# Moving work across the two ends of the attention stage in a fused attention, MLP and expert kernel

## The chip, the core and the metric

The kernel runs on one core of one Trainium2 chip. The metric is the device time of one execution in microseconds (us). Before the change the median of 3 runs is 1051.84 us (1050.31 to 1052.88). One further execution was taken with the hardware profiler: its own time is 1050.91 us, and the span that the trace covers is 1049.2 us.

## What is computed

Three layers run one after the other on 4 x 576 = 2304 tokens of width 512.

1. Attention with 8 heads of width 64 for each of 4 batches, causal, with a memory branch beside it:

```python
a = softmax(causal(q @ k.T / 8));  local = a @ v
q_p = phi(q)                       # phi(x) = max(x, 0) + exp(min(x, 0))
mem = (q_p @ M_prev) / (q_p @ z_prev + 1e-6)
g = sigmoid(beta)                  # one gate for each head
x = g * mem + (1 - g) * local
```

2. A gated MLP: `xn = x / sqrt(mean(x*x) + 1e-6) * rms_g`, then `(silu(xn @ w_gate) * (xn @ w_val)) @ w_out`, with an inner width of 1536. The three weight matrices arrive as 64-bit floats.

3. A mixture of 8 experts, each token going to its best one (512 to 1024 to 512), scaled by the router's probability and an output gate.

## The kernel before, in words

**Stages.** `attention` (L222) runs first. The MLP runs in `moe` (L923) over 5 blocks of 512 tokens (the last has 256), each in 12 steps f = 0..11 over 128 of the 1536 inner columns. The experts follow. Every large fp32 product is made of three fp32r products (high times high, high times low, low times high), so each weight tile is split into a rounded half and a rest: a copy and a subtraction.

**Attention.** Heads are taken two batches at a time (bp 0 and 1), so there are 16 heads n = 0..15, each in five units: four `Pair`s of 64-row blocks and one `Last`. The loop over units (L477 to L508) writes the order of the work by hand: at unit u it scores unit u on TensorE (PE) and takes the negative row maximum on VectorE (DVE), turns the weights of unit u-2 (PE transposes, ScalarE (ACT) copies), makes the exponentials of unit u (`soft`, ACT), and multiplies unit u-3 by v (`value`). After a head's last `value`, `add` scales the result (DVE, tile tm) and adds it to x on GpSimd (POOL). `recall` adds the memory branch at units 3 to 5 and at three units of every ten. `core.chain(True)` (L1152) holds this order on PE, DVE, ACT and POOL: an instruction there starts only after the one written before it on the same engine. The queue that issues DMAs (SP) is not held so; its order, and all orders after attention, are set by a scheduler at build time.

**Generators.** Side work is written as Python generators in a list `work`; at the end of each unit every generator is advanced by one `yield`. `load(n)` (L239) fetches q and k of head n and scales q by 0.125 on ACT, `phi(n)` (L248) fetches q again and makes phi(q) (DVE, ACT, DVE) for two heads, `piece` (L153) decodes one of 21 tiles of 64-bit weights to fp32 and stores it to DRAM (wgvd, woutd), `dense.weights` (L545) fetches the gate and value weights of one MLP step from wgvd and splits them, `rms` (L446) makes the mean squares of finished x rows (ACT, one row tile of 128 tokens at a time), the inverse root (POOL) and the scaled rows (DVE), and stores them to xd in DRAM. Before the change `rms` runs inside attention only for row tiles 0, 1, 2, 3 and 8 of bp 0 (`EARLY`); the other 4 row tiles of bp 0 and all 9 of bp 1 come in `late` (L513), which `moe` advances.

**The beginning.** Before unit 0 the DMAs of head 0, phi 0, the first v, beta and head 1 are issued (L278 to L285). Head 1's scaling on ACT (L246) and the gates `ig` = 1 + exp(-beta) and `io` = 1 + exp(beta) (L287 to L290) stand ahead of unit 0 on ACT and DVE. `ig` is first read by `recall` at unit 3, `io` by `add` after unit 4. phi's input tile q has one buffer.

**The end.** At the last unit of head 15, `route_constants` (L114) builds index constants on POOL and DVE: masks, ramps, and `ids`, 36 iotas of one column each. The weights of MLP step 0 are split during heads 12 and 13. After attention its SBUF pools are given back, and the pools of `moe` take the same memory. There `prepare(k)` (L949) fetches what step k needs: the weights (from step 1 on; from step 7 on `Late` decodes them in place) through tiles of tag `wo`, which has two buffers, and the output weights (`outw`, L937) through the same two buffers. `late` is advanced ten times before step 0 (L968), and four times in each step of block 0.

Of the kernel before, what the change touches and what calls it, by code (L numbers as in the profile page):

```python
# [17 lines left out]
P = 128  # L18
S = 576
# [17 lines left out]
EARLY = (0, 1, 2, 3, 8)  # L37
# [76 lines left out]
def route_constants(nc, cp, c):  # L114
# [28 lines left out]
    for bp in range(2):  # L143
        for t in range(9):
            for u in range(2):
                k = 8 * bp + t if t < 8 else 16 + bp
                nc.gpsimd.iota(ids[64 * u:64 * u + 64, k:k + 1], pattern=[[0, 1]], base=(2 * bp + (u ^ (t & 1))) * S + 64 * t, channel_multiplier=1)
# [74 lines left out]
def attention(ctx, nc, tc, ins, c, g8, rp, ps, xd, side):  # L222
# [16 lines left out]
    def load(n):  # L239

        qt = pl.tile([P, 2, S], F32, tag='qk', bufs=4, name='qt')
        heads.append(qt)
        nc.sync.dma_start(qt, qk[n // 8, n % 8].rearrange('b d (a s) -> (b d) a s', a=2))
        for _ in range(3 if n > 1 else 0):
            yield
        nc.scalar.mul(qt[:, 0], qt[:, 0], 0.125)  # L246

    def phi(n):  # L248

        q = pl.tile([P, 2, S], F32, tag='qs', bufs=1, name='q')  # L250
        nc.sync.dma_start(q, qs[n // 4, n % 4].rearrange('b p s -> p b s'))
        ph = pl.tile([P, 2, S], F32, tag='ph', name='ph')
        phis.append(ph)
        yield
        if n:
            yield
        nc.vector.tensor_scalar(ph, q, 0.0, None, op0=ALU.min)
        yield
        nc.scalar.activation(ph, ph, AF.Exp)
        yield  # L260
        nc.vector.scalar_tensor_tensor(ph, q, 0.0, ph, op0=ALU.max, op1=ALU.add)
# [18 lines left out]
    work = [phi(0)]  # L280
    next(work[0])
    values(0)
    nc.sync.dma_start(bt, ins['beta'].partition_broadcast(P))
    for _ in load(1):
        pass  # L285

    nc.vector.tensor_scalar(bt, bt, 80.0, -80.0, op0=ALU.min, op1=ALU.max)  # L287
    for t, sign in ((ig, -1.0), (io, 1.0)):
        nc.scalar.activation(t, bt, AF.Exp, scale=sign)
        nc.vector.tensor_scalar(t, t, 1.0, None, op0=ALU.add)  # L290
# [12 lines left out]
    def start(n):  # L303
# [7 lines left out]
        H.av = ps.tile([P, 8, 64], F32, tag='av', name='av')  # L311
        return H

    class Pair:
# [35 lines left out]
        def value(self):  # L350
            H, i = self.H, self.i
            for j in range(2):
# [5 lines left out]
    class Last:  # L358
# [35 lines left out]
        def value(self):  # L394
# [7 lines left out]
            if H.hh == 7 and H.bp == 0:  # L402
                work.append(rms(0, EARLY))

# [41 lines left out]
    def rms(bp, ts, ps=None):  # L446

        n = len(ts)
        x = [xs[bp][t // 4][:, t % 4] for t in ts]
        early = bp == 0 and ts[0] == 0  # L450
        pool = cp if early else rp
        ss, y, z = (pool.tile([P, 9], F32, tag=n + 'e' * early, name=n)[:, :len(ts)] for n in ('ss', 'y', 'z'))
# [3 lines left out]
        for t in range(n):  # L456
            sq = cp.tile([P, 512], F32, tag='sq', name='sq') if early else ps.tile([P, 512], F32, tag='m', name='sq')
            nc.scalar.activation(sq, x[t], AF.Square, accum_out=ss[:, t:t + 1])
            yield
        nc.vector.tensor_scalar(ss, ss, 1.0 / 512, 1e-6, op0=ALU.mult, op1=ALU.add)  # L460
        nc.gpsimd.tensor_tensor(y, ss, state['mhalf'][:, :n], op=ALU.pow)
# [51 lines left out]
    def late(ps):  # L513
        yield from rms(0, [t for t in range(9) if t not in EARLY], ps)
        yield from rms(1, range(9), ps)
# [407 lines left out]
def moe(ctx, tc, c, dense, X, late, g8, ps, ins, woutd, wr, rowd, wf, out):  # L923
# [25 lines left out]
    def prepare(k):  # L949
        if k < len(steps):  # L950
            bi, f = steps[k]
            if W[f] is None:
                for _ in dense.weights(f, g8 if f == 1 else w8, 'g8' if f == 1 else 'w8', pw, 'wo'):
                    pass
# [9 lines left out]
    ex = Experts(nc, c, wf, rowd, out, g8, w8, pw, pe, ps, cp)  # L964
    prepare(0)
    for p in range(2):
        decode.load(p)
    for _ in range(10):  # L968
        next(late)
# [10 lines left out]
    for k, (bi, f) in enumerate(steps):  # L980
# [7 lines left out]
        g = [ps.tile([P, 512], F32, tag='gv', bufs=3, name='gv')[:, :w] for _ in range(2)]  # L988
# [117 lines left out]
def body(tc, ins, out):  # L1106
# [4 lines left out]
    with ExitStack() as ctx:  # L1111
# [13 lines left out]
        with ExitStack() as c1:  # L1125
# [4 lines left out]
            def side(n, j):  # L1130
# [15 lines left out]
                if n == 12:  # L1146
                    w.append(dense.weights(0, g8, 'g8', pd, 'dw'))
                if n == 15:
# [53 lines left out]
```

## Time and profile before

| what | value |
|---|---|
| median of 3 runs | 1051.84 us |
| the profiled execution | 1050.91 us |
| its span | 1049.2 us |
| PE, DVE, ACT, POOL busy, share of the span | 93%, 66%, 54%, 24% |
| chain that ended last, PE's share | 62% |

Times within the trace are microseconds from the start of its span. In a timeline row the columns are start, duration, engine, source line, operation, what is written <- what is read, shape and count; brackets give the idle time of that engine just before, and what ended it. SPq is the queue that issues DMAs. PEld is the weight load that goes with a matmul. Most instructions carry line L57, since a helper there records them, so a row is found by its tile names: m are row maxima, mx those of a `Last`, a the attention weights, bt beta, qt the q and k of a head, ph phi(q), tm and x the attention output, Wf the split MLP weights, gv the first MLP product, dw and wo the tiles that weights are fetched to. A busy PE is not a PE at its peak, since matmuls overlap.

### The profile page before, as it was taken

What the parts mean: (1) busy time and instruction counts of PE and PEld (TensorE: products, weight loads), DVE (VectorE), ACT (ScalarE), POOL (GpSimd) and SP (SyncE); (2) the same over time, 40 slices, a digit from 0 to 9 for tenths busy, and PEclk for the clock granted to TensorE, in tenths of its full rate; (3) what the DMA queues carried; (4) which work ended last, traced back from release to release, by engine and by line L of the source; (5) the groups of instructions that cost most, each with busy time, mean ns of one, the idle gap of its engine ahead of it and who ended that gap; (6) DMA issues with size and microseconds to landing.
All of it is one profiled execution on the core that took longest, in us unless ns stands there. A gap on an engine that the chain in (4) does not pass through costs nothing.

```text
span 1049.2 us, 18572 instructions
## 1 busy us (share of the span) xinstructions
PE 974.8 (93%) x6727; PEld 751.7 (72%) x6727; DVE 693.7 (66%) x1261; ACT 571.3 (54%) x1113; POOL 251.1 (24%) x266
## 2 busy tenths in 40 slices
PE   5999998886989999999999999999879999999996
PEld 3666665554667777887788778888757888777785
DVE  3788888875987644234523354247687988888885
ACT  4788887766343332222222222235447888888885
POOL 1222222325555311110111112114003222222101
PEclk9999999998999999999999999999999999999999
DMA  8366556304754411021211112134134453387323
GB/s 275 100 203 193 180 180 223 101 25 161 261 170 123 135 44 61 31 71 32 69 31 51 31 61 67 35 96 147 60 101 154 128 195 125 101 297 272 101 101 98
DMA packets 51279, 128.21 MB, mean 122 GB/s; under 512 B 9965, under 2 KB 10477, under 8 KB 50672
## 3 DMA queue, kind: packets, MB, share of 16 engines
q1 hardware_dynamic: 47664, 116.48, 34.0%
q0 software_dynamic: 3520, 10.51, 3.1%
q8 instruction: 54, 0.88, 0.3%
q14 instruction: 41, 0.34, 0.1%
HBM read 160.50 MB, written 22.04 MB: 174 GB/s over the span
## 4 chain that ended last, share of the span: by engine, by line
PE 62%; DVE 12%; issue 8%; DMA 8%; ACT 6%; POOL 3%; SPq 0%; POOLq 0%; ACTq 0%; DVEq 0%
PE gv L57 22%; PE acc L57 11%; PE y L57 8%; PE h L57 7%; PE sc L57 3%; PE av L57 2%; PE tr L57 2%; DMA dw<-wgvd 2%; DMA out_dram<-ys,to 2%; DVE m L57 1%; PE tp L57 1%; ACT whl L850 1%; PE htp L57 1%; PE mp L57 1%; DVE whl L851 1%
## 5 line engine op out<-in xcount | busy, mean ns | idle before, releaser
L57 PE MATMUL gv<-xh,Wf 128*128 128x512 f32 (+1 forms) x960 | 290.1, 375 | 16.3 <-ACT Wf L57 7.8
L851 DVE TENSOR_TENSOR whl<-raw,whl 128x1024 fp32r<-128x1024 f32 x173 | 204.2, 1219 | 29.6 <-ACT whl L850 29.0
L57 PEld LDWEIGHTS gv<-xh,Wf 128*128 128x128 f32 x960 | 174.7, 189 | 51.9 <-ACT Wf L57 8.2
L850 ACT CAST whl<-raw 128x1024 fp32r<-128x1024 f32 x176 | 177.0, 1059 | 15.0 <-PE h L57 5.0
L57 PE MATMUL gv<-xl,Wf 128*128 128x512 f32 (+1 forms) x480 | 177.4, 370 | 0.0
L1007 POOL TENSOR_TENSOR sl<-th,sh 128x512 fp32r<-128x512 f32 (+1 forms) x58 | 72.3, 1246 | 313.0 <-ACT sh L1006 308.4
L57 PE MATMUL y<-whl,hh 128*128 128x512 f32 x528 | 137.7, 401 | 0.6 <-DVE whl L851 0.6
L57 PE MATMUL h<-whl,xgh 128*128 128x512 f32 x352 | 117.3, 401 | 2.7 <-DVE whl L851 2.0
L57 PEld LDWEIGHTS y<-whl,hh 128*128 128x128 f32 x528 | 97.4, 190 | 21.3 <-DVE whl L851 1.6
L57 PEld LDWEIGHTS gv<-xl,Wf 128*128 128x128 f32 x480 | 90.8, 189 | 14.2
L1006 ACT CAST sh<-th 128x512 fp32r<-128x512 f32 (+1 forms) x60 | 34.6, 576 | 121.2 <-DVE th L1003 121.2
L943 DVE TENSOR_TENSOR wol<-wo,woh 128x512 fp32r<-128x512 f32 x60 | 47.4, 789 | 67.6 <-ACT woh L942 67.5
L57 PE MATMUL acc<-woh,sh 128*128 128x512 f32 x216 | 87.1, 403 | 0.2
L57 PE MATMUL acc<-wol,sh 128*128 128x512 f32 x216 | 85.6, 396 | 0.0
L57 ACT ACTIVATE a<-sc,m 128x128 f32<-128x128 f32 (+3 forms) x128 | 66.9, 532 | 30.0 <-DVE m L57 18.6
L57 PE MATMUL acc<-woh,sl 128*128 128x512 f32 x216 | 78.8, 398 | 3.8 <-POOL sl L1007 3.8
L1002 DVE SCALAR_TENSOR_TENSOR th<-th,gv 128x512 f32<-128x512 f32 (+1 forms) x60 | 37.9, 632 | 63.4 <-ACT th L1001 63.3
L57 PEld LDWEIGHTS h<-whl,xgh 128*128 128x128 f32 x352 | 64.6, 188 | 21.1 <-DVE whl L851 7.4
L1001 ACT ACTIVATE th<-gv 128x512 f32<-128x512 f32 (+1 forms) x60 | 33.2, 554 | 83.0 <-PE gv L57 79.1
L942 ACT CAST woh<-wo 128x512 fp32r<-128x512 f32 x60 | 37.2, 620 | 64.8 <-PE acc L57 43.3
L1003 DVE TENSOR_TENSOR th<-th,gv 128x512 f32<-128x512 f32 (+1 forms) x60 | 37.9, 632 | 49.6 <-PE gv L57 49.0
L57 PE MATMUL h<-whl,xgl 128*128 128x512 f32 x176 | 68.7, 392 | 0.0
(252 smaller groups left out, 1571.3 us busy)
## 6 DMA issues: line engine op xcount, KB each, us to landing
raw<-in_wf_dram SPq DMA_DIRECT2D x168, 512.0 KB
wo<-woutd SPq DMA_DIRECT2D x60, 256.0 KB
raw<-in_wgv_dram SPq DMA_DIRECT2D x24, 512.0 KB
qt<-in_qk_dram SPq DMA_DIRECT2D x16, 576.0 KB
raw<-in_wout_dram SPq DMA_DIRECT2D x12, 512.0 KB
q<-in_qs_dram SPq DMA_DIRECT2D x8, 576.0 KB
xd<-x SPq DMA_DIRECT2D x18, 256.0 KB
rowd<-xr SPq DMA_DIRECT2D x4, 1028.0 KB
```

The lines of the kernel that those rows point to most:

```text
L57: i = call(*args, **kw).ins
L850: nc.scalar.copy(w[:, 0], src)
L851: (nc.gpsimd if k in pool_k else nc.vector).tensor_tensor(w[:, 1], src, w[:, 0].bitcast(F32), op=ALU.subtract)
L942: nc.scalar.copy(woh, wo)
L943: nc.vector.tensor_tensor(wol, wo, woh.bitcast(F32), op=ALU.subtract)
L1001: nc.scalar.activation(th, g[0], AF.Tanh, scale=0.5)
L1002: nc.vector.scalar_tensor_tensor(th, th, 1.0, g[0], op0=ALU.add, op1=ALU.mult)
L1003: nc.vector.tensor_tensor(th, th, g[1], op=ALU.mult)
L1006: nc.scalar.copy(sh, th)
L1007: (nc.vector if f >= 10 and bi == last else nc.gpsimd).tensor_tensor(sl, th, sh.bitcast(F32), op=ALU.subtract)
```

## The change

- The first scaling of head 1 waits three units, as for the later heads, so it stands behind unit 2's start; its DMA is issued before those of v and beta. phi's input tile q gets the pool's two buffers instead of one.
- The gates become a generator: the clamp and the two exponentials at unit 1, the two additions at unit 2.
- A head's PSUM tile av is created at its first `value` instead of at its start, which puts it behind the score tiles in PSUM; `moe` creates its first two gv tiles ahead of everything else.
- `rms(0)` takes all 9 row tiles of bp 0 inside attention; `late` is left with bp 1, and the ten advances ahead of step 0 are gone.
- The weights of MLP step 1 are fetched and split inside attention, one head after those of step 0.
- `route_constants` moves from head 15 to head 9, and `ids` is made by 12 iotas instead of 36.

```diff
     ids = t('ids', [NT], I32)
     for bp in range(2):
-        for t in range(9):
-            for u in range(2):
-                k = 8 * bp + t if t < 8 else 16 + bp
-                nc.gpsimd.iota(ids[64 * u:64 * u + 64, k:k + 1], pattern=[[0, 1]], base=(2 * bp + (u ^ (t & 1))) * S + 64 * t, channel_multiplier=1)
+        for u in range(2):
+            o, r = (2 * bp + u) * S, ids[64 * u:64 * u + 64]
+            nc.gpsimd.iota(r[:, 8 * bp:8 * bp + 8:2], pattern=[[P, 4]], base=o, channel_multiplier=1)
+            nc.gpsimd.iota(ids[64 * (1 - u):128 - 64 * u, 8 * bp + 1:8 * bp + 8:2], pattern=[[P, 4]], base=o + 64, channel_multiplier=1)
+            nc.gpsimd.iota(r[:, 16 + bp:17 + bp], pattern=[[0, 1]], base=o + 512, channel_multiplier=1)
...
-        for _ in range(3 if n > 1 else 0):
+        for _ in range(3 if n else 0):
             yield
         nc.scalar.mul(qt[:, 0], qt[:, 0], 0.125)
...
-        q = pl.tile([P, 2, S], F32, tag='qs', bufs=1, name='q')
+        q = pl.tile([P, 2, S], F32, tag='qs', name='q')
...
-    work = [phi(0)]
-    next(work[0])
+    work = [phi(0), load(1)]
+    for w in work:
+        next(w)
     values(0)
     nc.sync.dma_start(bt, ins['beta'].partition_broadcast(P))
-    for _ in load(1):
-        pass
-
-    nc.vector.tensor_scalar(bt, bt, 80.0, -80.0, op0=ALU.min, op1=ALU.max)
-    for t, sign in ((ig, -1.0), (io, 1.0)):
-        nc.scalar.activation(t, bt, AF.Exp, scale=sign)
-        nc.vector.tensor_scalar(t, t, 1.0, None, op0=ALU.add)
+
+    def gates():
+
+        yield
+        yield
+        nc.vector.tensor_scalar(bt, bt, 80.0, -80.0, op0=ALU.min, op1=ALU.max)
+        for t, sign in ((ig, -1.0), (io, 1.0)):
+            nc.scalar.activation(t, bt, AF.Exp, scale=sign)
+        yield
+        for t in (ig, io):
+            nc.vector.tensor_scalar(t, t, 1.0, None, op0=ALU.add)
+
+    work.append(gates())
+    next(work[-1])
...
-        H.av = ps.tile([P, 8, 64], F32, tag='av', name='av')
+        H.av = None
...
             H, i = self.H, self.i
+            if H.av is None:
+                H.av = ps.tile([P, 8, 64], F32, tag='av', name='av')
...
             if H.hh == 7 and H.bp == 0:
-                work.append(rms(0, EARLY))
+                work.append(rms(0))
...
-    def rms(bp, ts, ps=None):
-
-        n = len(ts)
+    def rms(bp, ps=None):
+
+        ts, n = (0, 1, 2, 3, 8, 4, 5, 6, 7), 9
...
-        yield from rms(0, [t for t in range(9) if t not in EARLY], ps)
-        yield from rms(1, range(9), ps)
+        yield from rms(1, ps)
...
-                for _ in dense.weights(f, g8 if f == 1 else w8, 'g8' if f == 1 else 'w8', pw, 'wo'):
+                for _ in dense.weights(f, w8, 'w8', pw, 'wo'):
...
     ex = Experts(nc, c, wf, rowd, out, g8, w8, pw, pe, ps, cp)
+    first = [ps.tile([P, 512], F32, tag='gv', bufs=3, name='gv') for _ in range(2)]
     prepare(0)
     for p in range(2):
         decode.load(p)
-    for _ in range(10):
-        next(late)
     prepare(1)
...
-        g = [ps.tile([P, 512], F32, tag='gv', bufs=3, name='gv')[:, :w] for _ in range(2)]
+        g = first if k == 0 else [ps.tile([P, 512], F32, tag='gv', bufs=3, name='gv')[:, :w] for _ in range(2)]
...
-                if n == 12:
-                    w.append(dense.weights(0, g8, 'g8', pd, 'dw'))
-                if n == 15:
+                if n in (12, 13):
+                    w.append(dense.weights(n - 12, g8, 'g8', pd, 'dw'))
+                if n == 9:
                     route_constants(core, cp, c)
```

## Rows read from the trace of the kernel before

**Rows 1.** The profile page, busy time of each engine over the span.

```profile
PE 974.8 (93%) x6727; PEld 751.7 (72%) x6727; DVE 693.7 (66%) x1261; ACT 571.3 (54%) x1113; POOL 251.1 (24%) x266
```

**Rows 2.** Busy time by stretch: attention, block 0, and 10 us of it.

```profile
core 0: us, PE busy (x) PEld busy (x) DVE busy (x) ACT busy (x) POOL busy (x), PEclk, DMA share, GB/s
13.00:241.20 228.20, 208.09 (x3068) 138.23 (x3068) 182.29 (x389) 172.75 (x507) 64.27 (x102) 0.99 0.49 159
246.60:363.80 117.20, 99.54 (x417) 75.94 (x416) 92.92 (x142) 47.97 (x89) 54.29 (x39) 0.97 0.54 177
250.00:260.00 10.00, 4.46 (x11) 3.13 (x12) 8.13 (x15) 8.24 (x21) 3.29 (x3) 0.66 0.67 248
```

**Rows 3.** Timeline of all engines, the first 30 us.

```profile
6.44 0.39 PE L57 MATMUL sc<-maskb,identb 128*128 128x128 bf16 x2
...
9.41 0.17 DVE L57 TENSOR_SCALAR bt<-bt 128x8 f32<-128x8 f32 x1 [5.00 <-DMA bt<-in_beta_dram]
...
12.00 0.68 ACT L57 ACTIVATE qt<-qt 128x576 f32<-128x576 f32 x1 [6.24 <-DMA qt<-in_qk_dram]
...
12.99 0.42 DVE L57 TENSOR_REDUCE m<-sc 128x2 f32<-128x256 f32 x1
...
15.80 0.69 DVE L57 TENSOR_REDUCE m<-sc 128x2 f32<-128x512 f32 x1 [0.86 <-PE sc L57]
...
18.68 0.38 SPq L251 DMA_DIRECT2D q<-in_qs_dram  x1
...
24.15 0.76 DVE L57 TENSOR_SCALAR ph<-q 128x1152 f32<-128x1152 f32 x1 [1.95 <-DMA q<-in_qs_dram]
...
24.83 0.75 DVE L57 TENSOR_REDUCE mx<-scl 128x2 f32<-128x576 f32 x1
```

**Rows 4.** Timeline of POOL, heads 5, 7, 9 and 11 added to x, and attention's end.

```profile
101.49 1.88 POOL L57 TENSOR_TENSOR x<-x,tm 128x256 f32<-128x256 f32 x3 [1.55 <-DVE tm L57]
...
128.04 1.87 POOL L57 TENSOR_TENSOR x<-x,tm 128x256 f32<-128x256 f32 x3 [1.59 <-DVE tm L57]
...
156.07 2.32 POOL L57 TENSOR_TENSOR x<-x,tm 128x256 f32<-128x256 f32 x3 [4.47 <-DVE tm L57]
...
184.01 1.89 POOL L57 TENSOR_TENSOR x<-x,tm 128x256 f32<-128x256 f32 x3 [4.58 <-DVE tm L57]
...
236.91 6.62 POOL L57 IOTA ids<- 64x1 int32 x36
...
244.85 1.71 POOL L57 TENSOR_TENSOR x<-x,tm 128x256 f32<-128x256 f32 x3
```

**Rows 5.** Groups by line and form, DVE and ACT, 100 to 246 us; last numbers: busy, mean ns.

```profile
L57 DVE TENSOR_SCALAR x<-x,y 128x512 f32<-128x512 f32 x5 | 3.6, 715 | 0.0
...
L57 DVE TENSOR_TENSOR Wf<-dw,Wf 128x512 fp32r<-128x512 f32 x1 | 0.7, 693 | 0.0
L57 DVE CAST Wf<-dw 128x512 fp32r<-128x512 f32 x1 | 0.4, 417 | 0.0
L57 DVE CAST lane<-lane_i 128x128 f32<-128x128 int32 x1 | 0.2, 221 | 0.0
...
L57 ACT ACTIVATE sq<-x 128x512 f32<-128x512 f32 x9 | 5.6, 622 | 2.6 <-DVE tm L57 1.5 <-POOL x L57 0.9
```

**Rows 6.** Timeline of DVE and PE, attention's end and MLP step 1's first product.

```profile
237.54 0.42 DVE L57 TENSOR_SCALAR sq<-dt 128x512 int32<-128x512 int32 x1
...
241.22 0.28 DVE L57 TENSOR_SCALAR tm<-avl,r 128x64 f32<-128x64 f32 x1
...
255.06 0.80 PE L57 MATMUL gv<-xh,Wf 128*128 128x512 f32 x1 [7.78 <-ACT Wf L57]
```

**Rows 7.** Timeline of DVE and POOL in block 0: weights of steps 1, 6, 11 split.

```profile
258.04 0.68 DVE L57 TENSOR_TENSOR Wf<-dw,Wf 128x512 fp32r<-128x512 f32 x1
...
310.08 1.19 DVE L57 TENSOR_TENSOR Wf<-dw,Wf 128x512 fp32r<-128x512 f32 x1
...
351.79 1.48 POOL L219 TENSOR_TENSOR Wf<-sq,Wf 128x512 fp32r<-128x512 f32 x1
```

More of the change, by code (lines that the diff above doesn't have):

```diff
@@ L36 @@
 XL, XT = (12, 2), ((14, 0), (14, 2), (14, 4), (15, 1))
-EARLY = (0, 1, 2, 3, 8)
 NEARLY = 4
@@ L444, in add @@
             nc.gpsimd.tensor_tensor(xv, xv, tm[:, 4 * u:min(4 * u + 4, 9)], op=ALU.add)
-    def rms(bp, ts, ps=None):
-        n = len(ts)
+    def rms(bp, ps=None):
+        ts, n = (0, 1, 2, 3, 8, 4, 5, 6, 7), 9
         x = [xs[bp][t // 4][:, t % 4] for t in ts]
-        early = bp == 0 and ts[0] == 0
-        pool = cp if early else rp
-        ss, y, z = (pool.tile([P, 9], F32, tag=n + 'e' * early, name=n)[:, :len(ts)] for n in ('ss', 'y', 'z'))
+        pool = rp if bp else cp
+        ss, y, z = (pool.tile([P, 9], F32, tag=f'{n}{bp}', name=n) for n in ('ss', 'y', 'z'))
         if 'mhalf' not in state:
@@ L456, in rms @@
         for t in range(n):
-            sq = cp.tile([P, 512], F32, tag='sq', name='sq') if early else ps.tile([P, 512], F32, tag='m', name='sq')
+            sq = cp.tile([P, 512], F32, tag='sq', name='sq') if not bp else ps.tile([P, 512], F32, tag='m', name='sq')
             nc.scalar.activation(sq, x[t], AF.Square, accum_out=ss[:, t:t + 1])
@@ L460, in rms @@
         nc.vector.tensor_scalar(ss, ss, 1.0 / 512, 1e-6, op0=ALU.mult, op1=ALU.add)
-        nc.gpsimd.tensor_tensor(y, ss, state['mhalf'][:, :n], op=ALU.pow)
+        nc.gpsimd.tensor_tensor(y, ss, state['mhalf'], op=ALU.pow)
         yield
```

## The prediction

> **What bounds the kernel now.** I read the page first, then busy time by stretch, then the timelines of the two ends of attention. On the page PE is busy for 93% of the span [rows 1], so time can come only from stretches where PE stands or waits in lockstep with others. The stretches show three such places [rows 2]. In attention (13 to 241 us) PE, DVE and ACT are busy for 91%, 80% and 76% of 228 us: no single engine is full, each unit hands over from one to the next. Before 13 us there is hardly any work on DVE and ACT. In block 0 of the MLP PE is busy for 99.5 of 117.2 us: 17.7 us of idle time. The later blocks and the experts are not touched; whatever moves the start of block 1 moves the end by as much.
>
> **The start.** The scores of unit 0 are done at 6.83 us, but their maximum is taken at 12.99 [rows 3]. Between them stand the gates: the clamp waits for beta until 9.41, and the gates' exponentials stand on ACT behind the scaling of head 1, which waits for its DMA until 12.00 [rows 3]. A second wait follows: the second phi's DMA is issued only at 18.68, when the single q buffer is free, and DVE waits for it until 24.15, ahead of unit 4's maximum at 24.83 [rows 3].
>
> After the change unit 0's maximum can go at about 7, a gain of 6. But the clamp now stands at unit 1, and behind it on DVE wait unit 2's maximum, behind that unit 2's exponentials on ACT and its transposes on PE. Beta's DMA is issued behind head 1's now. The DMAs carry the same bytes in another order, so I take beta to land where head 1 landed, at about 12; the other end is where it landed before, 9.4. Unit 2's maximum, at 15.80 before, then goes at 12: a gain of 3.8. From there to unit 4's maximum it was 9.03 us, 1.95 of them the wait for the second phi [rows 3]. With q's second buffer that DMA goes out right behind head 2's, by 13 instead of 18.68, and took 5.4 us to land, so it is there at about 18.4, when unit 4 comes up: 3.8 + 1.95 = 5.8. If beta lands at 9.4 the whole 6 of unit 0 is kept, with the second wait 8. I take 6.5, nearer the first, as head 1's 576 KB do go ahead of beta; the lower bound is 4, unit 2's gain alone. What is late next is the lockstep of the three engines. Head 1's scaling on ACT, 0.68 [rows 3], only moves from before unit 0 to unit 2. On SP the second phi's 576 KB go ahead of loads that are needed five units later.
>
> **What is moved into attention.** The nearest price is the same work already there: five row tiles of `rms(0)`. Two heads take 26.55 us without it (101.49 to 128.04), then 28.03 and 27.94 with it [rows 4], so five row tiles cost 2.87 us. Their passes alone are 5 x (0.62 on ACT + 0.72 on DVE) = 6.7 us [rows 5], so 0.43 of the work shows. The four new row tiles: 2.3 us. Step 1's weights put one pass on ACT (0.6, taken as the square's), a cast of 0.42 and a subtraction of 0.69 on DVE; the constants put nine small DVE operations of about 0.2 there [rows 5], in all 3.5 us; at 0.43 that is 1.5. Their DMAs (two loads, four stores) stand on SP three or more units ahead of their readers, as those of step 0 do. Sum: +3.5 us. The bounds: nothing, and all of it in series, 4 x 1.34 + 3.5 = 8.9.
>
> On POOL come a subtraction of 1.5 (step 11's takes 1.48 [rows 7]) and the constants, with 12 iotas at 6.62 / 36 = 0.18 [rows 4], 2.2 us. A DVE operation at 237.54, inside the burst of iotas, took 0.42 us, as the cast of a tile of the same size does [rows 4 to 6], so I charge nothing for POOL. The Trainium skill ("SBUF — State Buffer", section "Who interferes with whom") speaks against this: some forms of DVE operation (casts and tensor_scalar among them) and GpSimd operations lock each other out for a whole instruction. By it the POOL work would hold DVE for up to its own length, and the sum would come out 3.7 us higher; the row under the iotas does not show it, and no row here tests the subtraction.
>
> **Attention's end and block 0.** Heads end on DVE at 241.50 [rows 6], but the last addition on POOL ends at 246.56 [rows 4], since 36 iotas (6.62 us) stand in front. With them gone it ends about 1.9 us after DVE, as the additions of heads 5 to 11 did: 243.4, so attention's memory is handed over 3 us earlier. The split, placed in attention, of step 1's weights removes the worst wait: PE waits 7.78 us for them at 255.06 [rows 6], and runs part of the next stretch at a low clock (0.66 granted on average from 250 to 260 [rows 2]).
>
> What replaces that wait? Two chains start at the handover. (a) The two `wo` buffers: each step needs three loads through them, and the second halves of the weights of steps 1 to 6 are done at 258.04 to 310.08, one step in 10.4 us [rows 7], more than the 8.3 us that PE needs (99.5 / 12). Without step 1 in this ring everything in it comes one period earlier: 10.4 + 3 = 13.4 us. (b) The decoder of steps 7 to 11 ends at 353.3 [rows 7]; step 11's second half starts on PE 5.5 us ahead of 363.8, at 358.3. It gains the 3 us and the DVE time that leaves block 0: 4 x 0.72 + 0.42 + 0.69 + about 0.8 for the small ones = 4.8, in all 7.8, and it had 5 us in hand: 12.8. (c) PE's idle time allows 17.7. The least is 12.8; I take 12.5, since DVE, at 92.9 busy of 117.2 us [rows 2], would have to be busy for 88.1 of 104.7. Below, only the 3 and 4.8 us show and the wait moves to step 2: 7.8; above, 16.
>
> **Edits at nothing.** av's place in PSUM and the early gv tiles only change which banks are waited for; PE starts gv at the 241.5 that DVE sets, and a start up to 0.4 us earlier or later is inside the rounding. If the scheduler lets gv run ahead of the last heads' products instead, the handover is late by those products, which is rival B's case.
>
> **Sum.** -6.5 + 3.5 - 12.5 = -15.5 us on the profiled execution's 1050.91: 1035.4. The median of the runs is 0.93 higher, so 1036.3; I forecast **1036 us**.
>
> **The rivals.**
> A is the forecast: 1036, own range 1032 to 1041.
> B: **the wait moves to step 2.** The ring or the handover hold block 0 as before, only 7.8 us come back: 1036.3 + 4.7 = 1041. For it: the ring's period is above PE's step. Against it: a whole period leaves the ring.
> C: **the moved work is hidden and the block fills up.** -7.5 + 1 - 15 = -21.5: 1030. For it: 17.7 us of idle PE. Against it: five row tiles did show.
> D: **POOL holds DVE.** The added 3.7 us of POOL work go wholly on DVE's path: 1040. The rule of the Trainium skill above is this one. Against it: the 0.42 us operation among the iotas. For it: in the stretch itself POOL was busy for 64 us [rows 2] and its share in the 0.43 can't be read off.
> E: **slower: lockstep takes the moved work in full.** In attention, units 49 to 73, all of it goes in series on ACT, DVE and POOL, 8.9 + 3.7 = 12.6 us, and the units also wait for it on PE. It decides from the point where that is above the gain of the two ends, 11.8 at their lower bounds (4 + 7.8). With half as much again for the handovers between engines, 18.9 - 11.8 = +7: 1059. Against it: the 0.43 of the rows above.
> F: **the change doesn't do what it says:** step 1's weights are still late, because their buffer is one that x's rows held and is not yet free, so the 7.78 us wait stays. -6.5 + 3.5 - 3 = -6: 1046. Against it: those rows are stored some ten units before.
>
> **Chances.** A 0.53, B 0.21, C 0.11, D 0.05, E 0.05, F 0.05. A difference of 0.3% (3.2 us) is about what a measurement of this kernel can tell from no change. Faster by more: A, B, C, D and most of F, less their low ends (start 4, block 7.8, moved work 8.9 would give 1049): 0.90. Within it: 0.05. Slower: E, 0.05. The range runs from C to just short of F: 1030 to 1045.
>
> **What would show each step.** Right: unit 0's maximum near 7 us, unit 4's near 18.3; the second phi's DMA issued by 13 and hardly waited for; pairs of heads with `rms` no longer than 30 us; the last addition on POOL within 2.5 us of the last tm; no PE wait above 2 us at step 1; block 1's first gv starting about 15 us before its old 363.8. Wrong: a wait for beta of more than 5 us at unit 1; PE waiting at steps 2 to 6 for Wf as long as it did at step 1; ACT or DVE standing at the moved weights; a low granted clock at a new place in attention.

## The result, and the profile of the changed kernel

The changed kernel takes 1039.14 us (median of four runs, 1037.81 to 1043.70) against 1052.36 us (four runs, 1050.31 to 1053.41): a ratio of 0.9881, 95% interval 0.9862 to 0.9901. That is 1.2% less, 3 us above the forecast of 1036 us and inside its range of 1030 to 1045. A later repeat, in five rounds, gave 1041.33 against 1053.40 us: 0.9891 (0.9874 to 0.9907). The profiled execution took 1039.59 us with a span of 1037.9; before it was 1050.91 with 1049.2.

The page's engine line hardly moves against [rows 1]: the same work stands in a span that is 11 us shorter.

```profile
PE 974.7 (94%) x6727; PEld 752.1 (72%) x6727; DVE 696.3 (67%) x1256; ACT 569.8 (55%) x1113; POOL 248.8 (24%) x241
```

Busy time by stretch, the counterparts of [rows 2]: attention from 13 us to its last tm, block 0 from the last x addition to block 1's first gv, and ten microseconds of block 0.

```profile
core 0: us, PE busy (x) PEld busy (x) DVE busy (x) ACT busy (x) POOL busy (x), PEclk, DMA share, GB/s
13.00:235.60 222.60, 203.73 (x3037) 136.04 (x3032) 185.03 (x392) 171.62 (x504) 65.72 (x93) 0.98 0.55 174
237.40:348.20 110.80, 101.71 (x432) 78.28 (x431) 89.50 (x131) 45.66 (x85) 53.91 (x38) 1.00 0.50 164
244.00:254.00 10.00, 10.00 (x47) 8.17 (x46) 8.32 (x15) 5.83 (x12) 7.98 (x5) 1.00 0.37 110
```

Block 0 is 6.4 us shorter (110.80 against 117.20). In the ten microseconds in which PE was idle for more than half the time at a granted clock of 0.66, it is now busy throughout at full clock.

The start, timelines of DVE, SP's queue and POOL, beside [rows 3]:

```profile
6.59 0.42 DVE L56 TENSOR_REDUCE m<-sc 128x2 f32<-128x256 f32 x1 [2.19 <-PE sc L56]
...
9.68 0.43 SPq L251 DMA_DIRECT2D q<-in_qs_dram  x1
...
10.18 0.17 DVE L56 TENSOR_SCALAR bt<-bt 128x8 f32<-128x8 f32 x1 [0.82 <-DMA bt<-in_beta_dram]
10.26 0.68 DVE L56 TENSOR_REDUCE m<-sc 128x2 f32<-128x512 f32 x1
...
15.49 0.76 DVE L56 TENSOR_SCALAR ph<-q 128x1152 f32<-128x1152 f32 x1 [0.25 <-DMA q<-in_qs_dram]
16.17 0.75 DVE L56 TENSOR_REDUCE mx<-scl 128x2 f32<-128x576 f32 x1
...
27.36 1.92 POOL L56 TENSOR_TENSOR x<-x,tm 128x256 f32<-128x256 f32 x3 [23.23 <-DVE tm L56]
```

Unit 0's maximum comes at 6.59 (12.99 before), unit 2's at 10.26 (15.80), unit 4's at 16.17 (24.83). Head 0 is added to x at 27.36, before at 36.01: **8.65 us** earlier. Head 5 (92.86) and head 7 (119.42) keep 8.63 and 8.62 of it [rows 4].

Heads 7 and 11 added to x, the 12 iotas between them, attention's end and the handover, timelines of POOL and DVE, beside [rows 4, 6]:

```profile
119.42 1.87 POOL L56 TENSOR_TENSOR x<-x,tm 128x256 f32<-128x256 f32 x3 [1.60 <-DVE tm L56]
...
137.34 2.21 POOL L56 IOTA ids<- 64x4 int32 x12
...
176.97 1.88 POOL L56 TENSOR_TENSOR x<-x,tm 128x256 f32<-128x256 f32 x3 [4.47 <-DVE tm L56]
...
235.60 0.28 DVE L56 TENSOR_SCALAR tm<-avl,r 128x64 f32<-128x64 f32 x1
235.65 1.70 POOL L56 TENSOR_TENSOR x<-x,tm 128x256 f32<-128x256 f32 x3 [2.07 <-DVE tm L56]
```

The last tm starts at 235.60 against 241.22, so 3.03 of the 8.65 us went into attention. The last addition on POOL ends 1.46 us after the last tm; before it was 5.06.

PE's waits in block 0 from there to 270 us, beside PE's wait of 7.78 in [rows 6]:

```profile
235.94 0.50 PE L56 MATMUL gv<-xh,Wf 128*128 128x512 f32 x1 [0.39 <-DVE tm L56]
259.03 0.50 PE L56 MATMUL gv<-xh,Wf 128*128 128x512 f32 x1 [0.35 <-ACT Wf L56]
...
260.53 0.73 PE L56 MATMUL gv<-xh,Wf 128*128 128x512 f32 x2 [0.76 <-POOL Wf L56]
264.06 0.50 PE L56 MATMUL gv<-xh,Wf 128*128 128x512 f32 x1 [0.97 <-DVE Wf L56]
265.86 0.73 PE L56 MATMUL gv<-xh,Wf 128*128 128x512 f32 x2 [1.07 <-DVE Wf L56]
```

The wait at step 1 is gone. What is late next are the weights of the steps after it, a microsecond at a time. Block 1's first gv starts at 348.07 instead of 363.77, and the first row of block 1's output leaves PSUM at 462.20 instead of 477.86. This last row is the marker used below, since it has the same wait for PE's last product in every profile:

```profile
462.20 0.60 ACT L590 ACTIVATE xr<-acc 128x512 f32<-128x512 f32 x1 [2.76 <-PE acc L56]
```

It is 15.66 us earlier. At the same place of blocks 2 and 3 the 15.66 still stand (569.97 and 674.80, before 585.63 and 690.46). Then 1.4 us go in the last block and 2.1 among the experts, and the last tile for the store is made at 1029.58, 12.17 us ahead of 1041.75.

### The profile page after: what moved, and what is told of

Same layout as the page of the kernel before. It is cut to its first block, busy times and chain, and to the rows that moved or that the text cites. A ratio compares the mean times of both kernels' runs of the same rounds, so it can differ in the third digit from the quotient of the medians.

```text
span 1037.9 us, 18552 instructions
## 1 busy us (share of the span) xinstructions
PE 974.7 (94%) x6727; PEld 752.1 (72%) x6727; DVE 696.3 (67%) x1256; ACT 569.8 (55%) x1113; POOL 248.8 (24%) x241
## 4 chain that ended last, share of the span: by engine, by line
PE 60%; DVE 14%; issue 8%; DMA 7%; ACT 7%; POOL 2%; SPq 0%; ACTq 0%; POOLq 0%; DVEq 0%
PE gv L56 22%; PE acc L56 11%; PE y L56 9%; PE h L56 7%; DMA out_dram<-ys,to 2%; DVE m L56 2%; PE av L56 2%; PE sc L56 2%; PE tr L56 2%; DMA wo<-woutd 1%; PE tp L56 1%; ACT whl L858 1%; PE htp L56 1%; DVE whl L859 1%; DVE dt L56 1%
## 5 line engine op out<-in xcount | busy, mean ns | idle before, releaser
L951 DVE TENSOR_TENSOR wol<-wo,woh 128x512 fp32r<-128x512 f32 x60 | 45.0, 751 | 70.3 <-ACT woh L950 70.3
```

The lines of the kernel that those rows point to most:

```text
L951: nc.vector.tensor_tensor(wol, wo, woh.bitcast(F32), op=ALU.subtract)
```

## The experiments

To keep apart what belongs to which stretch, each profile is read at three points: where the first x addition on POOL ends (the start), from there to the end of the last tm (attention), and from there to block 1's first output row, as above (handover, block 0 and block 1, whose own steps no kernel here changes). "x lag" is the end of the last x addition behind the last tm. All are sums and differences of timeline rows. The time is that of the profiled execution.

| kernel | start | attention | x lag | last tm to block 1's row | time |
|---|---|---|---|---|---|
| before | 37.93 | 203.57 | 5.06 | 236.36 | 1050.91 |
| changed | 29.28 | 206.60 | 1.46 | 226.32 | 1039.59 |
| changed, again | 29.24 | 207.66 | 1.46 | 226.50 | 1037.40 |
| start undone | 37.16 | 206.52 | 1.46 | 227.40 | 1045.39 |
| one q buffer | 38.81 | 206.19 | 1.48 | 226.74 | 1046.09 |
| gates first | 32.83 | 207.69 | 1.48 | 226.20 | 1040.70 |
| step 1's weights undone | 29.79 | 208.23 | 1.45 | 231.10 | 1046.86 |
| weights and rows undone | 29.10 | 204.47 | 1.46 | 230.03 | 1037.64 |
| 12 iotas at the end | 28.76 | 206.56 | 1.47 | 226.57 | 1036.26 |
| 36 iotas at the end | 31.64 | 208.09 | 5.05 | 228.44 | 1043.81 |
| nearly the start alone | 29.81 | 203.75 | 4.88 | 233.70 | 1042.14 |
| PSUM places undone | 30.06 | 209.14 | 1.46 | 225.91 | 1038.84 |
| no decoder arithmetic | 29.96 | 209.22 | 1.48 | 218.58 | not read |
| work from DVE to ACT | 30.11 | 209.17 | 1.46 | 224.97 | 1039.59 |

Each row is one profile of one execution, and the stretch behind the last tm has a limit of its own: the order of its instructions is set when the kernel is built. In seven rows (changed, again, start undone, one q buffer, gates first, 12 iotas at the end, PSUM places undone) that order is the same: of DVE's instructions in the 112 us from the last tm, told apart by operation, tiles and shape, 99% or more stand in one common order. These seven run from 225.91 to 227.40. The other edits of the changed kernel change the order too. DVE's agrees with the changed kernel's in 82% (36 iotas), 73% (DVE to ACT), 69% (weights undone), 63% (weights and rows undone) and 58% (no decoder arithmetic). What such an edit is worth can't be told apart from what its new order is worth, and "Nearly the start alone" below suggests that an order can be worth 2.7 us.

### The changed kernel again

> The changed kernel itself, timed beside the others on the same chip. Expected 1039 us as before, ratio to the kernel before 0.988; the first row of block 1's output leaves PSUM within 1.5 us of 462.2. It shows what two profiles of one kernel differ by.

The last column but one agrees within 0.2 us, the start within 0.04. Attention differs by 1.06 us, and the time by over 2 us. Where: the granted clock. Three stretches of attention, first of the profile above, then of the repeat (columns as in the windows above, the granted clock third from the end):

```profile
183.00:190.00 7.00, 4.98 (x81) 3.25 (x83) 4.52 (x9) 6.80 (x20) 0.00 (x0) 1.00 0.08 29
204.00:211.00 7.00, 4.32 (x39) 2.01 (x38) 4.97 (x11) 3.62 (x11) 2.39 (x4) 0.76 0.00 1
221.00:228.00 7.00, 5.36 (x50) 2.81 (x48) 4.95 (x11) 4.10 (x14) 1.84 (x3) 0.76 0.49 150
```

```profile
183.00:190.00 7.00, 5.16 (x63) 3.79 (x66) 3.11 (x5) 6.37 (x19) 0.00 (x0) 0.76 0.07 26
207.00:214.00 7.00, 4.64 (x30) 2.66 (x32) 5.43 (x11) 4.28 (x13) 2.95 (x4) 0.76 0.00 0
221.00:228.00 7.00, 5.43 (x88) 3.46 (x84) 4.95 (x11) 5.52 (x19) 0.82 (x2) 1.00 0.42 150
```

A mean of 0.76 over 7 us means that PE ran for about half of them at 1.2 GHz instead of 2.4. Which places fall is not fixed by the kernel: the first and the third row changed places. Three kernels above with nearly the changed attention (PSUM places, no decoder arithmetic, DVE to ACT) had a third such place at 155 to 162 us (0.76 there in the first of them), and all three have an attention of 209.14 to 209.22 us. So an attention read from one profile is uncertain by some 2.6 us, and where parts of it are compared below, the places are named.

The repeat keeps its gain whole up to the last tile: its marker is 14.46 us ahead of the kernel before, its last tile (1027.30) 14.45; its span is 13.6 us shorter.

### The start undone

Edit, the lines of the kernel before put back (the gates too, as in the diff above):

```
-    work = [phi(0), load(1)]
+    work = [phi(0)]
...
+    for _ in load(1):
+        pass
...
-        q = pl.tile([P, 2, S], F32, tag='qs', name='q')
+        q = pl.tile([P, 2, S], F32, tag='qs', bufs=1, name='q')
```

> The changed kernel with its whole start undone: the gates and the scaling of head 1 stand ahead of unit 0 again, and there is one q buffer; attention's inside and end stay as changed. Theory (the start's gain is carried whole through the lockstep and through block 0): unit 0's maximum back near 13 us, unit 4's near 24.8, every later marker of the changed kernel's trace about 8.6 us later: the last tm ends at 244.5 (changed kernel 235.9), block 1's first gv starts at 356.9 (348.2), time 1039 + 8.6 = 1048. Rival (the tail of attention or block 0 is bounded by something that starts on its own clock, a DMA chain for instance, and swallows part): the last tm under 242, or block 1's first gv under 354, and a time under 1045.

The first x addition ends 7.88 us later (37.16), the last tm 7.80, block 1's first gv starts at 356.98 as the theory has it (8.91 later), the marker is 8.88 later (471.08). Nothing is swallowed, neither by attention nor by block 0. The time rose by less (1045.39, where the theory had 1048), since the profile it is compared with lost 3.5 us behind the marker, and this one 0.6.

### One q buffer, and the gates first

The two halves of the start, each by itself: `bufs=1` for q and phi with everything else as changed, and the gates' lines put back ahead of unit 0 with everything else as changed.

> The changed kernel with one buffer for q and phi instead of two; the gates and the second head's scaling stay behind the first units. Theory (two separate waits, the second 1.95 us in the kernel before): unit 0's maximum stays near 6.6, the second phi's DMA is issued only when q is free, at about 12.5, and DVE waits 2 us or more for it; the first x addition ends 2 to 2.7 us later than in the changed kernel (31.3 to 32, against 29.3), and all later markers by as much. Rival (the earlier first units free q early enough): the wait is under 0.5 us and all markers are within 0.5 us of the changed kernel's, so that the whole 8.65 comes from the gates and head 1.

> The changed kernel with the gates ahead of unit 0 again, while head 1's scaling stays behind the first units and q keeps its two buffers. With one buffer and the gates late nothing was left of the start's gain, so the second phi's DMA counts for all of it in that direction. Theory (the two are a maximum, not a sum: unit 4 goes when both the units before it and the second phi are there): beta lands at 10.2, unit 0's maximum at about 11, unit 4's at 20 to 21 (16.2 in the changed kernel), the first x addition ends at 33 to 34, some 4 us later than in the changed kernel. Rival (only the second phi counts): unit 4's maximum within 1 us of 16.2.

With one buffer the theory's wait is there, but with four times its size. SP's queue and DVE:

```profile
16.80 0.38 SPq L251 DMA_DIRECT2D q<-in_qs_dram  x1
...
25.02 0.76 DVE L56 TENSOR_SCALAR ph<-q 128x1152 f32<-128x1152 f32 x1 [8.74 <-DMA q<-in_qs_dram]
```

The second phi's DMA is issued 1.9 us earlier than before [rows 3], but takes 8.2 us until DVE has it instead of 5.5. In front of it stand eight other loads, issued from 10.23 to 14.66 us, that stand behind it in the changed kernel. The same eight stand in front of it in the kernel before (11.36 to 15.25) and with the start undone (10.46 to 14.33), where it was issued at 18.68 and 17.83 and used at 24.15 and 23.38. In all three the DMA engines are busy nearly throughout from 14 to 24 us (a share of 0.97 to 1.01), and the earlier issue behind those loads brought nothing. DVE waits 8.74 us for it, and the start ends at 38.81: **none of the 8.65 us is left**. With the gates first, DVE:

```profile
10.30 0.17 DVE L56 TENSOR_SCALAR bt<-bt 128x8 f32<-128x8 f32 x1 [5.90 <-DMA bt<-in_beta_dram]
...
11.00 0.42 DVE L56 TENSOR_REDUCE m<-sc 128x2 f32<-128x256 f32 x1
...
19.71 0.75 DVE L56 TENSOR_REDUCE mx<-scl 128x2 f32<-128x576 f32 x1
```

Unit 0 waits for beta as forecast (11.00), unit 4 comes at 19.71 (forecast 20 to 21), and 5.1 of the 8.65 us are there (32.83). So the late gates and head 1's late scaling with one buffer give -0.9, the second buffer and head 1's late scaling with early gates 5.1, all together 8.65. That is how the later of two chains behaves, and not a sum of two waits. (The late scaling of head 1 was not undone by itself; each combination is one profile.) The kernel with 36 iotas shows it once more, by chance: its second phi landed late, at 17.86, DVE waited 2.34 us for it, and its start is 2.4 us later than the changed kernel's with the same code.

### Step 1's weights, and the four rows, behind attention again

```
-                if n in (12, 13):
-                    w.append(dense.weights(n - 12, g8, 'g8', pd, 'dw'))
+                if n == 12:
+                    w.append(dense.weights(0, g8, 'g8', pd, 'dw'))
...
-                for _ in dense.weights(f, w8, 'w8', pw, 'wo'):
+                for _ in dense.weights(f, g8 if f == 1 else w8, 'g8' if f == 1 else 'w8', pw, 'wo'):
```

The second kernel also has `rms(0, (0, 1, 2, 3, 8))` inside attention and `rms(0, (4, 5, 6, 7), ps)` in front of `rms(1)`, as before.

> The changed kernel with one part undone: the weights of step 1 are loaded and split behind attention again, through the same two buffers as those of the later steps; all nine rows' scaling of the first block and the constants stay inside attention. Theory of the ring (block 0 is paced by three loads per step through two buffers, one period of 10.4 us): attention ends 1.4 us earlier (last tm 234.5), PE waits 6 us or more for the second half of step 1's weights, and block 1's first gv starts at 348.2 - 1.4 + 10.4 = 357. Rival (block 0 is paced by the decoder and DVE's queue, the wait at step 1 was slack that came back later): 0.42 + 0.69 of DVE work return, block 1's first gv at 347 to 353.

> The changed kernel with two parts undone: step 1's weights behind attention again, and of the first block's rows four are scaled behind attention again. Only the constants and the start stay changed. Attention ends about 3 us earlier than in the changed kernel (last tm 232.9). Theory one (the wait at step 1 and the four rows' DVE work hold block 0 as they did before): handover at 234.4 and 117.2 us from there as before, so block 1's first gv at 351.6 and a time of 1042. Theory two (the four rows' work was under cover in block 0): no later than the kernel in which the weights alone are undone, less 1.6 us. Theory three (both cost more behind attention since the decoder starts behind them): block 1's first gv above 355.

With the weights alone undone, the stretch behind the last tm takes 4.78 us more (231.10); block 1's first gv starts at 355.00, between the two theories. PE's waits, and ten microseconds of it:

```profile
247.58 0.77 PE L56 MATMUL acc<-woh,sh 128*128 128x512 f32 x1 [3.75 <-ACT sh L1013]
265.61 0.51 PE L56 MATMUL gv<-xh,Wf 128*128 128x512 f32 x1 [3.82 <-DVE th L1009]
```

```profile
244.00:254.00 10.00, 6.42 (x17) 5.12 (x18) 8.44 (x11) 4.19 (x10) 5.68 (x4) 0.66 0.76 247
```

With the weights inside attention block 0 is 4.8 us shorter: a wait and the low clock behind it go (0.66, as before the change; 1.00 with the weights inside). That is clear of the 1.5 us by which kernels of one order differ, though the order differs here too. The gain is not the ring's whole period of 10.4. Nor does PE wait for the ring's weights themselves: it waits for ACT's and DVE's work on the products of steps 0 and 1, which stands in their queues behind passes of the decoder and of the x rows. Attention was not shorter than in the changed kernel, though the theory of the ring had its end 1.4 us earlier; the clock hides what the weights cost there. They cost 0.9 us, from this profile's 208.23 against the 209.14 to 209.22 of the kernels with the same three places of low clock.

With the four rows behind attention as well, block 0 does not get longer: 230.03, 1.07 less. Block 1's first gv starts at 349.49, as theory two has it: the rows' work was under cover there. In attention the rows and the weights together cost 2.13 us (206.60 less 204.47). Some 0.5 of these belong to the clock: the changed kernel has a second place of low clock at 224.5, which this profile and the repeat don't have, and from head 13's addition to head 15's it takes 27.94 us where the repeat takes 27.47. So moving rows and weights brings 3.71 - 2.13 = 1.6 us net, or about 2 without that place. That is less than an order can be worth: this kernel's marker, 463.60, is 1.40 us behind that of the changed kernel but 0.20 behind that of its repeat, and its time, 1037.64, is no higher. That moving them brings anything is not shown.

### The constants

```
-                if n == 9:
+                if n == 15:
```

and, in the second kernel, the 36 iotas of before in place of the 12.

> The changed kernel with the constants at their old place, the last unit pair but with 12 iotas instead of 36. Theory (the place does not matter once there are only 12, 2.2 us on POOL instead of 6.6): the last x addition on POOL ends within 2.5 us of the last tm, handover, block 1's first gv (348.2) and time as in the changed kernel within 1 us. Rival (POOL's burst stands in front of the last additions wherever it is in the last pair): the last x addition ends 3 us or more behind the last tm, and block 1's first gv up to 3.8 us later.

> The changed kernel with the constants as in the kernel before: 36 iotas, made in the last pair of heads; all else as changed. Theory (the burst stands in front of the last additions on POOL, and block 0 starts at the last of them): the last x addition ends about 5 us behind the last tm (1.5 in the changed kernel), and the first row of block 1's output leaves PSUM 3.6 us later than in the changed kernel, 465.8 against 462.2, time up by as much. Rival (the handover is under cover, since block 0 is paced by its weight loads and by DVE): that row at most 1.5 us later, under 463.7.

With 12 iotas the place makes no difference: lag 1.47, marker 461.89, 0.3 us from the changed kernel's. The last additions no longer stand behind the burst; POOL, first of this kernel, then of the one with 36:

```profile
230.72 2.52 POOL L56 IOTA ids<- 64x4 int32 x12
235.08 1.71 POOL L56 TENSOR_TENSOR x<-x,tm 128x256 f32<-128x256 f32 x3 [0.48 <-DVE tm L56]
```

```profile
235.15 6.60 POOL L56 IOTA ids<- 64x1 int32 x36
241.83 1.29 POOL L56 TENSOR_TENSOR sq<-dt,sq 128x512 f32<-128x512 f32 x1
243.07 1.71 POOL L56 TENSOR_TENSOR x<-x,tm 128x256 f32<-128x256 f32 x3
```

With 36 the additions are 3.6 us later behind the last tm, of which 2.1 reach the marker (228.44 against 226.32): a part of the handover's delay is covered in block 0. (The order differs here, and PE runs at a granted clock of 0.66 from 270 to 280 us, where the changed kernel keeps full clock.) The marker itself (468.17) is later by more, by the late second phi and the low clock in attention.

### Nearly the start alone, and the places in PSUM

The first kernel is that with weights and rows undone, with 36 iotas at the end as well; of the change it has the start and the places of av and of the first gv tiles. The second undoes those places alone (`H.av` taken at the start of a head, no `first`).

> Nearly the kernel before: only the start is changed, with av's and the first gv tiles' places in PSUM; the constants (36 iotas), the four rows' scaling and step 1's weights are where they were. Theory (the start is additive and the places in PSUM are worth nothing): every marker from unit 4 on 8.65 us ahead of the kernel before: last tm 232.9, last x addition 237.9, the first row of block 1's output leaves PSUM at 469.2 (before 477.9), time 1043. Rival one (attention's end or block 0 swallows part of an earlier start): that row after 471.5. Rival two (the places in PSUM let PE run ahead in block 0): that row before 467.5.

> The changed kernel with the PSUM places as before: av's tile taken at the start of a head, the first gv tiles not taken ahead of the first prepared weights. Theory (in the run with nearly the start alone block 0 came 2.5 us earlier than the start explains, so the places are worth that): the first row of block 1's output leaves PSUM 2 to 3 us later than in the changed kernel, 464.2 to 465.2. Rival (the 2.5 us are what two profiles differ by): within 1 us of 462.2.

The first has the old wait again, at PE:

```profile
246.87 0.79 PE L56 MATMUL gv<-xh,Wf 128*128 128x512 f32 x1 [7.50 <-ACT Wf L56]
```

Still its stretch behind the last tm is 233.70, 2.66 us shorter than before. So its marker, 467.26, is rival two's. But in the changed kernel the places bring nothing: without them it has 225.91, 0.4 us less than with them. (Its marker, 465.11, looks like the theory's; but the 2.9 us come from the start and from attention's third place of low clock.) What else differs is the order of the instructions, which an edit elsewhere shifts in block 0 too: of DVE's instructions there 78% stand in the same order as before. So the 2.66 us most likely come with the order, perhaps by way of the places; an order was not tried by itself.

### What holds block 0

```
         nc.scalar.activation(sq, hw.bitcast(F32), AF.Copy, scale=float(2.0 ** -112))
-        nc.vector.tensor_scalar(t, sq.bitcast(I32), 3, None, op0=ALU.logical_shift_left)
...
-        nc.gpsimd.tensor_tensor(sq, t.bitcast(F32), sq, op=ALU.add)
```

> The changed kernel with the decoder of the weights of steps 7 to 11 cut to its first pass on ACT: its four DVE passes (45 us of DVE's 91 in block 0) and its addition on POOL (21.5 us) are left out, so those weights are not decoded; the loads, the splits and the stores stay. Theory (what holds block 0 above PE's 108 us of work is DVE's queue): PE's waits between 255 and 345 go and the first row of block 1's output leaves PSUM 5 us or more earlier than in the changed kernel's trace, under 457.2. Rival (it is held by the loads through the two output-weight buffers): the waits at steps 2 to 6 stay and that row comes less than 2 us earlier, above 460.2.

The routes of the tokens follow from those weights, so only the stretch to the marker is read: 218.58, 7.74 us shorter (the marker is at 457.76, just above the 457.2 that the theory asked for, after an attention of 209.22). Busy time over 107.5 us from the last x addition on, of this kernel and of the changed one:

```profile
240.50:348.00 107.50, 104.20 (x452) 83.84 (x451) 51.98 (x75) 48.02 (x89) 31.92 (x24) 0.98 0.54 181
```

```profile
237.20:344.70 107.50, 98.41 (x418) 75.63 (x417) 87.27 (x127) 45.01 (x84) 52.36 (x37) 1.00 0.51 167
```

PE is idle for 3.3 us instead of 9.1, with the same loads through the same two buffers. So it is mostly the work on DVE and POOL, and not the ring, that holds block 0. The kernel made from that, which also has the 12 iotas in the last pair of heads:

```
-            nc.vector.tensor_scalar(x[j], x[j], y[:, j:j + 1], None, op0=ALU.mult)
+            if bp:
+                nc.scalar.activation(x[j], x[j], AF.Copy, scale=y[:, j:j + 1])
+            else:
+                nc.vector.tensor_scalar(x[j], x[j], y[:, j:j + 1], None, op0=ALU.mult)
...
-            if u:
+            if u and dtag != 'wo':
...
-                if n == 9:
+                if n == 15:
```

> The changed kernel with work taken from DVE in block 0: the second rows' nine multiplications by the inverse norm go on ACT, the two casts per step there are both on ACT, and the 12 iotas stand in the last pair of heads. Theory (DVE's queue is what holds block 0 above PE's work; without the decoder's 45 us it was 7.8 us shorter): DVE loses 9 x 0.7 + 5 x 0.74 = 10 us of its 90, ACT (46 of 111 busy) takes them; in proportion to the 45 us the first row of block 1's output comes 1.5 to 2.5 us earlier than in the changed kernel (462.2), 460 to 461, time 1.5 to 2.5 us lower. Rival (ACT's queue waits for the raw weights' loads and the x rows now wait behind it): block 1's second rows are late, that row comes at 462 or later.

The stretch is 224.97, 1.35 us shorter than the changed kernel's and 1.53 shorter than its repeat's: the theory's lower end, and 0.9 below the least of the seven kernels of one order, but with another order of its own. By the marker alone, 464.25, the rival would have it (462 or later); it stands behind an attention of 209.17. Over five rounds its median is 1038.76 us, a ratio to the kernel before of 0.9856 (0.9837 to 0.9874); the changed kernel's on the same chip is 0.9891 (0.9874 to 0.9907). The two intervals just touch: probably better, by some 2.6 us (1041.33 less 1038.76), and not settled.

## Why the prediction was right, and where it wasn't

The time, the sign and the places of the gain held; the sum came out by luck as well. The terms added up to -15.5 us; measured at the marker it is -15.66, but two terms missed by 2 us or more, in opposite directions (2.15 too little, 2.46 too much). One of the prediction's own signs of being wrong was there too: a low granted clock at new places in attention (at 224.5 us; in the repeat at 186.5).

**The start: forecast -6.5 (bounds 4 to 8), measured -8.65, above both bounds.** The step "I take beta to land where head 1 landed, at about 12" failed: it landed at 10.2. So unit 2 gained 5.5 us, not 3.8. From unit 2's maximum to unit 4's the prediction took off the 1.95 us of DVE's wait for the second phi; it became 5.91 instead of 9.03, 3.1 less. And the sum of two waits was the wrong form: the two partial edits behave as the maximum of two chains does (-0.9 and 5.1, all 8.65). The wait of 1.95 in [rows 3] was only what the second phi was late behind an already late unit 4; without the second buffer it grows to 8.74 when the rest is early. Why it is 3.1 and not 1.95 that went between units 2 and 4 is not shown.

**Moved into attention: forecast +3.5, measured +3.03.** The prediction's own terms, 2.3 for the rows and 1.5 for weights and constants, add up to 3.8 and not to 3.5. The agreement is partly luck: in the repeat attention is 4.1 us longer than before, and in the three kernels with a third place of low clock 5.6. Head by head the price from the neighbouring heads (0.43 of the passes) was too high where rows and constants stand: from head 7 to head 11 the changed kernel takes 57.55 us (119.42 to 176.97), before it was 55.97 [rows 4], so 1.6 us for what was put at 2.3 and 0.8 (0.43 of nine operations of 0.2). The weights cost 0.9 for 0.7 (0.43 of 1.7), and some 0.5 came with the clock. Heads 9 to 11 take 30.1 us (146.87 to 176.97), against the 30 given as a limit.

**Attention's end and block 0: forecast -12.5, measured -10.04** (226.32 against 236.36 from the last tm). Taken step by step from the kernel before (236.36, 233.70, 230.03, 231.10, 226.32) 2.7 came with nearly the start alone, so most likely with the build's order, 3.7 with the constants (2.1 in the other comparison), -1.1 with the rows and 4.8 with the weights, each with an order of its own. The handover itself was as forecast, 3.6 us for 3. The step that failed is chain (a), "everything in it comes one period earlier", together with the 2.9 us of DVE time in chain (b) for the rows: the block is held by DVE and POOL, where the rows were under cover, and most of PE's idle time of 9.1 us there is still theirs (3.3 are left without the decoder's work). The bounds of 7.8 to 16 took it in.

**"Whatever moves the start of block 1 moves the end by as much"** held in the repeat (14.46 to 14.45) and lost 3.5 us in the first profile. There the granted clock was 0.84 from 724 to 735 us, and ACT waited longer for the weights of the last expert tiles (2.26 us, then 1.40; in the repeat 1.77 and then no more):

```profile
1020.06 1.05 ACT L858 CAST whl<-raw 128x1024 fp32r<-128x1024 f32 x1 [2.26 <-DMA raw<-in_wf_dram]
```

The 3 us between 1036 and the median can't be split further: executions of the changed kernel lie between 1037.40 and 1043.70, and two of them have a trace.

**The rivals.** B (the wait moves to step 2) is there in small: 0.35 to 1.07 us at each of the next waits, not 7.8. C did not come: PE keeps 9.1 us of idle time. E is excluded by the +3.03 (5.6 at most), F by PE's row at 235.94, after which no wait of 0.3 us or more follows until 259.03. D's mechanism is seen in the rows of the last section; attention got 3.03 us longer in all, so at most a part of that is D's.

## What to carry to other kernels

Where several loads and waits stand at a start, list for each unit everything that must be there, and take the latest; undoing one of two edits then costs more than its share, and the other alone may bring nothing. Moving work out of a stretch helps by what that stretch's queue is short of, not by the length of the work or of the visible wait: here a wait of 7.8 us with a low clock behind it gave 4.8, four row passes gave nothing, and less what they cost in attention the two brought 1.6 us, which is not clear of what an order brings. Shortening a burst on a side engine, here 36 instructions to 12, took 3.6 us from the handover, of which 2.1 or more stayed, and with 12 its place no longer mattered. Where the order of instructions is set at build time, a difference between two builds holds that order too: compare the orders before giving the time to an edit.

## What the runs showed of the hardware that was not expected

DVE's instructions stretch beside POOL's. A cast of a 128x512 tile takes 0.41 us in block 0 with nothing on POOL. Timeline of DVE and POOL of the changed kernel:

```profile
267.92 1.31 POOL L211 TENSOR_TENSOR sq<-dt,sq 128x512 f32<-128x512 f32 x1 [0.63 <-DVE sq L210]
267.95 0.69 DVE L1009 SCALAR_TENSOR_TENSOR th<-th,gv 128x512 f32<-128x512 f32 x1
...
273.99 1.31 POOL L1014 TENSOR_TENSOR sl<-th,sh 128x512 fp32r<-128x512 f32 x1 [2.72 <-ACT sh L1013]
274.05 1.52 DVE L56 CAST Wf<-dw 128x512 fp32r<-128x512 f32 x1 [0.57 <-DMA dw<-wgvd]
...
275.24 1.49 POOL L211 TENSOR_TENSOR sq<-dt,sq 128x512 f32<-128x512 f32 x1
275.61 1.67 DVE L56 TENSOR_TENSOR Wf<-dw,Wf 128x512 fp32r<-128x512 f32 x1
```

The cast ends 0.27 us after POOL's subtraction, the DVE subtraction (0.68 elsewhere) 0.55 after POOL's addition: each seems to have done its work when POOL was through. In block 0 of the changed kernel 21 DVE instructions on 128x512 with POOL beside them take 18.8 us longer, in sum, than the shortest of their form (22 and 20.7 us before), of some 90 us that DVE is busy; the 72 of that size with nothing on POOL are all within 0.02 us of the shortest. Those that read the product in PSUM don't stretch: the first DVE row above has POOL beside it from end to end and takes 0.69, and all 24 of them in block 0 take 0.67 to 0.69. That is in line with the Trainium skill ("SBUF — State Buffer", section "Who interferes with whom"): of a DVE cast or an operation with two inputs in SBUF and a GpSimd operation that reads SBUF, the later one waits for the whole of the earlier. In attention from head 5 on the same reckoning gives 10.5 us, against 7.1 before: it may be part of what the moved work costs. The prediction took the 0.42 us operation under the iotas [rows 4, 6] as evidence against it; but an iota is short, 0.18 us, and what stands beside iotas says nothing of POOL's subtractions and additions of 1.3 us and more. DVE's stretching would also explain how the kernel without decoder arithmetic gains on two engines at once; a kernel with POOL's work alone taken out was not tried.

The granted clock falls at different places in different executions of the same code (186.5 and 210.4 us in one, 207.4 and 224.5 in the other). The two executions of the changed kernel differ there by 1.1 us, the kernels with nearly the same attention and a third place from the first of them by 2.6.
